# Loading the third input pair ahead of the token weights, and beginning the token product one slot early, in a fused retention and wave-MLP kernel

## Chip, cores and metric

One core of a Trainium2 chip. The metric is device time in microseconds (us), the median of some runs of one kernel. Some executions fall in a slow state with a lower granted clock (the TensorE clock that the profile records, as a share of the full one): a run more than 1.5% above the fastest of its kernel counts as slow, and ratios use the fast runs alone. A profiled run has a span that is about 1.7 us shorter than its device time; all times inside a kernel are from the start of that span. L12 is line 12 of the kernel; the change adds lines, so L340 of the kernel before is L349 after, L368 is L377, L400 is L409, L312 is L317, L322 is L331, L347 is L356, L375 is L384.

## The reference

```python
# q, k, v: (4, 8, 768, 64), float32
state = gamma * state + outer(k[t], v[t])        # per batch and head, over 768 steps
x[t]  = q[t] @ state / 8                         # heads side by side: x is (4, 768, 512)
theta = x @ w_theta
y = w_tok_r @ (x * cos(theta)) + w_tok_i @ (x * sin(theta))   # over the 768 tokens
u = x + y
out = u + max(u @ w_ch, 0)
```

## The kernel before

The retention is done in chunks of 128 tokens. A **pair** n is two chunks of one batch (3 pairs a batch, 12 in all): k and q are flipped (transposed) by TensorE into kqT, A = k q is masked by VectorE, Y = A v and the product with the state (I) add up to yT, S adds k v to the state. ScalarE or VectorE copies yT to xT; theta is a matmul of xT, ScalarE makes cosine and sine, VectorE makes z = x cos, x sin. M is the token product of one tile of 128 tokens (12 matmuls, six per weight); u = x + y; U flips u; O is the channel product; "ot" is the result. The token weights must be cast and flipped too: "w flip".

The engines take their instructions in the order in which the program writes them (the prediction gives the page and the trace line for it). What matters here are the buffers in PSUM, into which the matmuls of this kernel write, and the order in one turn of the loop, which I call **slot** n:

```python
def flip(n, name, copy=nc.vector.tensor_copy):          # 8 transposes, one copy
    ps = psum.tile([P, 2, NP, P], BF, name="kq_ps", tag="tr", bufs=2)
def x_pe(n, copy=...):   x_ps = psum.tile(..., tag="tr", bufs=2)
def moe_U(ms):           u_ps = psum.tile(..., tag="tr", bufs=2)     # read by ScalarE
def moe_O(m):            o_ps = psum.tile(..., tag="tr", bufs=2)     # read by VectorE
def w_flip(r, t0):       w_ps = psum.tile(..., tag="tr", bufs=2)     # r=0: VectorE, r=1: ScalarE
def theta(n, a):         th_ps = psum.tile(..., tag="acc", bufs=2)   # yT_ps of ret_Y has this tag too
def moe_M(m, lo, hi):    y_ps = psum.tile(..., tag="y", bufs=1)
...
# slots 4 and 5 (n), one tile "first" each; cut to the order
ret_I(n-1, 1); ret_A(n, 0); ret_mask(n, 0); ret_Y(n-1, 1); ret_S(n-1, 1)
ret_out(n-1, 0); ret_out(n-1, 1)           # yT -> xT, ScalarE
moe_M(first, 0, 2)                         # stands in the wait for xT
theta(n-1, 0); x_pe(n-1); theta(n-1, 1)    # preps(DP): q half VectorE, half GpSimd, about here
flip(n+1, "k")
ret_S(n, 0); ret_A(n, 1); ret_mask(n, 1); ret_Y(n, 0); ret_I(n, 0); moe_U(done)
moe_M(first, 2, 4)
w_tok(n)                                   # two w flips, between them on VectorE zmul(n-1, .)
moe_M(first, 4, nT); flip(n+1, "q"); moe_u(first)    # slot 5: this q flip stands behind the k flip
moe_O(done); moe_out(done)
```

Of the kernel before, what the change touches and what calls it, by code (L numbers as in the profile page):

```python
# [14 lines left out]
FT = mybir.dt.float32  # L15
BF = mybir.dt.bfloat16
# [16 lines left out]
def kernel(  # L33
# [17 lines left out]
    nc = tc.nc  # L51
# [39 lines left out]

    def load_wtok(r, t0):
        src = (moe_w_tok_r, moe_w_tok_i)[r]
        t = io.tile([P, S], FT, name="wtok", bufs=4)
        nc.sync.dma_start(out=t, in_=src[t0 * P:(t0 + 1) * P, :])
        wdma[r, t0] = t

    def loads(order):
        for what in order.split():
            if what == "th":  # L100
                load_w512("th", moe_w_theta)
            elif what == "ch":
                load_w512("ch", moe_w_ch)
            elif what[0] == "w":
                for r in range(2):
                    load_wtok(r, int(what[1:]))
            else:
                for name in "kqv":
                    load(int(what[1:]), name)

    loads("p0 th p1 w0 p2 w1 w2 p3 w3 ch p4 w4 p5 w5")


    warm = const.tile([P, dm], BF)
# [72 lines left out]
            copy(t, ps)  # L187
        st[n, name + "T"], st[n, name + "_ps"] = t, ps

    def flip_out(n, name):  # L190
        nc.vector.tensor_copy(st[n, name + "T"], st[n, name + "_ps"])

    def flip_dma(n, name):
        t = work.tile([P, 2, NP, P], BF, name="kqT", bufs=6)
# [109 lines left out]
    def x_out(n, copy):  # L304
        b, g = divmod(n, nG)
        copy(xs[b][:, 2 * g:2 * g + 2, :],
             st[n, "x_ps"].rearrange("p a j e -> p a (j e)"))

    def theta(n, a):
        th_ps = psum.tile([P, dm], FT, name="th_ps", tag="acc", bufs=2)  # L310
        for j in range(NP):
            nc.tensor.matmul(th_ps, st[n, "xT"][:, a, j, :], wth[:, j, :], start=(j == 0),  # L312
                             stop=(j == NP - 1))
        cs = work.tile([P, 2, dm], BF, name="cs", bufs=3)
        nc.scalar.activation(cs[:, 0, :], th_ps, AF.Sin, bias=halfpi, scale=1.0)  # L315
        nc.scalar.activation(cs[:, 1, :], th_ps, AF.Sin, bias=zerob, scale=1.0)  # L316
        st[n, "cs", a] = cs  # L317
# [53 lines left out]

    def moe_out(m):
        b, t0 = divmod(m, nT)
        ot = work.tile([P, dm], FT, name="ot", bufs=8)
        nc.vector.scalar_tensor_tensor(ot, mo[m]["o"], 0.0, mo[m]["u"], ALU.max, ALU.add)  # L375
        mo[m]["ot"] = ot

# [3 lines left out]

    wrow = {}

    def w_cast(t0):  # L384
        for r in range(2):
            row = work.tile([P, S], BF, name="wrow", bufs=5)
            nc.gpsimd.tensor_copy(row, wdma[r, t0])  # L387
            wrow[r, t0] = row

    def w_flip(r, t0, copy=True):  # L390
# [12 lines left out]
    def w_tok(t0):  # L403
        for r in range(2):
            w_flip(r, t0)
# [56 lines left out]
    def keep_busy(times):  # L462
        for _ in range(times):
            nc.tensor.matmul(warm_ps, warm[:, 0:P], warm, start=True, stop=True)
# [35 lines left out]
    theta(0, 1)  # L500
    flip(1, "q")
    prep(1, "v", PP)
    w_cast(0)
    x_pe(0, None)
    ret_A(1, 0)
    ret_mask(1, 0)
    x_out(0, DV.tensor_copy)
    keep_busy(3)
    ret_S(1, 0)
    state_out(1, 0)  # L510
# [1 line left out]
    ret_mask(1, 1)  # L512
    ret_Y(1, 0)
    ret_I(1, 0)
    w_flip(0, 0)
    ret_S(1, 1)
    state_out(1, 1)
    ret_I(1, 1)
    ret_Y(1, 1)
    ret_out(1, 0, AC.copy)  # L520
    ret_out(1, 1, DV.tensor_copy)
    w_flip(1, 0)
    prep(2, "k", (PL,))
    zmul(0, 0)
    flip(2, "k")
    prep(2, "q", DP)
    theta(1, 0)
    zmul(0, 1)
    theta(1, 1)
    moe_M(0, 0, 1)  # L530
    flip(2, "q")
    prep(2, "v", PP)
    w_cast(1)
    w_cast(2)
    x_pe(1, AC.copy)
    moe_M(0, 1, 2)
    ret_A(2, 0)
    ret_mask(2, 0)
    ret_S(2, 0)
    state_out(2, 0)  # L540
    ret_A(2, 1)
    ret_mask(2, 1)
    zmul(1, 0)
    ret_Y(2, 0)
    ret_I(2, 0)
    ret_I(2, 1)
    w_flip(0, 1, False)
    w_flip(1, 1, False)
    ret_Y(2, 1)
    ret_out(2, 0, AC.copy)  # L550
    ret_out(2, 1, DV.tensor_copy)
    w_out(0, 1)
    w_out(1, 1)
    zmul(1, 1)
    prep(3, "k", (PL,))
    moe_M(0, 2, 3)
    theta(2, 0)
    flip(3, "k")
    prep(3, "q", DP)
    theta(2, 1)  # L560
    moe_M(0, 3, 4)
    x_pe(2)
    w_flip(0, 2, False)
    w_out(0, 2, AC.copy)
    moe_M(1, 0, 2)
    zmul(2, 0)
    flip(3, "q")
    prep(3, "v", PP)
    w_cast(3)
    moe_M(1, 2, 4)  # L570
    zmul(2, 1)
    moe_M(0, 4, 5)


    tiles_of = {nG - 2: [], nG - 1: [0, 1]}
# [16 lines left out]
    for n in range(nG, B * nG + 1):  # L592
        mine, done = tiles_of[n], tiles_of[n - 1]
        late, two = n > nG, len(mine) > 1
        nxt = n + 1 in pairs

        if nxt and n + 1 >= K_DMA:
            flip_dma(n + 1, "k")
        if nxt and n + 1 >= Q_DMA:
            flip_dma(n + 1, "q")  # L600
        if n <= X_DMA and n + 3 in pairs:
            load(n + 3, "k")
        if n >= U_DMA:
            moe_U_dma(done[1])
        def preps(engines):
            prep(n + 1, "q", engines)
            prep(n + 1, "v", PP)
            if n in (nG, nG + 1):
                w_cast(n - nG + 4)

        if n == nG:
            nc.gpsimd.tensor_copy(wch, wdma["ch"])
        if nG + 3 < n + 1 < Q_DMA:
            preps(PP)
        if late:
            ret_I(n - 1, 1)

        if n in pairs:
            ret_A(n, 0)
            ret_mask(n, 0)  # L620
        if n == nG:
            moe_M(0, 5, nT)
            w_flip(1, 2)
            moe_u(0)
            moe_M(1, 4, nT)
            moe_u(1)
        if late:
            ret_Y(n - 1, 1)
            ret_S(n - 1, 1)
            ret_out(n - 1, 0, nc.scalar.copy)  # L630
            ret_out(n - 1, 1, nc.scalar.copy)
            state_out(n - 1, 1)
            if n < nG + 3:
                prep(n + 1, "k", (PL,))
                if n > nG + 1:
                    preps(DP)
            if n - 1 >= X_DMA:
                x_dma(n - 1)
        if n > X_DMA and n + 3 in pairs:
            load(n + 3, "k")  # L640
        if n + 3 in pairs:
            load(n + 3, "q")

        first = mine[0]
        moe_M(first, 0, 3 if two else 2)
        if late:
            theta(n - 1, 0)
            if n - 1 < X_DMA:
                x_pe(n - 1)
            if n == nG + 1:  # L650
                preps(DP)
            theta(n - 1, 1)
        if two:
            moe_M(first, 3, nT)
            moe_u(first)
        for name, limit in (("k", K_DMA), ("q", Q_DMA)):
            if nxt and nG + 1 < n + 1 < limit and (n > nG + 1 or name == "k"):
                flip(n + 1, name)
        if n + 1 >= K_DMA and not two:
            moe_M(first, 2, 4)  # L660
        if n + 3 in pairs:
            load(n + 3, "v")
        for t in stores_in(n):
            store(t)
        if n + 1 >= U_DMA:
            moe_U_dma(first)

        if n in pairs:
            ret_S(n, 0)
            state_out(n, 0)  # L670
            ret_A(n, 1)
            ret_mask(n, 1)
            ret_Y(n, 0)
            ret_I(n, 0)
        if n < U_DMA:
            moe_U(done)
        if n == nG:
            prep(n + 1, "k", (AC,))
            preps(DP)
        if n == nG or n + 1 < K_DMA and not two:  # L680
            moe_M(first, 2, 4)
        early_z = late and n < nG + 3
        if early_z and n > nG + 1:
            zmul(n - 1, 0)
        if n < nG + 3:
            w_tok(n - nG + 3)
        if early_z:
            zmul(n - 1, 0 if n == nG + 1 else 1)
        if not two:
            moe_M(first, 4, nT)  # L690
            if n == nG + 1:
                flip(n + 1, "q")
            moe_u(first)
            if n == nG + 1:
                zmul(n - 1, 1)
        elif n in pairs:
            moe_M(mine[1], 0, nT)
        if n + 2 in pairs and n > nG + 1:
            prep(n + 2, "k", (AC,))
        if n + 2 in pairs and n + 2 >= Q_DMA:  # L700
            prep(n + 2, "q", PP)
            prep(n + 2, "v", PP)
        if two and n in pairs:
            moe_u(mine[1])
        for i, t in enumerate(done):
            if n == nG:
                flip(n + 1, "kq"[i])
            moe_O(t)
            moe_out(t)
        if late and not early_z:  # L710
            zmul(n - 1, 0)
            zmul(n - 1, 1)
        if n not in pairs:
            moe_M(mine[1], 0, nT)
            moe_u(mine[1])
# [43 lines left out]
```

## Time and profile before

| kernel before | |
|---|---|
| time, median of 3 runs | 168.55 us (168.35 to 169.74) |
| span of the profiled run | 166.5 us, granted clock 1.00 |
| prologue, to A of pair 3 | 38.25 us |
| slots 3, 4, 5, 6 | 10.16, 10.22, 10.20, 7.76 us |
| slot 7 begins | 76.59 us |

Slot boundaries are read off TensorE in order of time: the first state product (L245) of each slot. The lines are in the prediction. Two more: all that TensorE waited for theta and for Y over the whole run, from the list of waits (engine, line, releaser, us in total, times, longest):

```profile
PE th_ps L312 <- ACT xT L285: 0.3, 1, 0.3
PE yT_ps L231 <- ACT cs L316: 0.3, 1, 0.3
```

### The profile page before, as it was taken

The page shows a single profiled execution, that of the slowest core. Times are in us where ns is not written, and L with a number is a line of the kernel's source. Part 1 is how long each engine was busy: PE and PEld are TensorE (multiplying, and loading weights), DVE is VectorE, ACT ScalarE, POOL GpSimd, SP SyncE. Part 2 cuts the span into 40 slices and gives each one's busy share as a digit, 9 for nine tenths or more (in the row PEclk, how much of TensorE's full clock was granted, in tenths as well). Part 3 has the DMA queues.
Part 4 walks back from the last instruction along what each step waited for, and adds up shares of the span by engine and source line. Part 5 has one row for each costly group of instructions (what it writes and reads, how often), then busy time and mean ns, then how long its engine had stood idle before and what let it go on. Part 6 is the DMA issues. An engine that isn't in the chain of part 4 may idle for free.

```text
span 166.5 us, 4614 instructions
## 1 busy us (share of the span) xinstructions
PE 155.2 (93%) x1933; PEld 87.2 (52%) x1959; DVE 102.4 (61%) x137; ACT 79.1 (48%) x137; POOL 66.6 (40%) x82
## 2 busy tenths in 40 slices
PE   6969897899999999999999999999999999999991
PEld 2345664664755667555555554455545444444460
DVE  2257798878686699939446464584554736334442
ACT  7216568371819467687847827447083350000010
POOL 6275959786685877771442703600000000000000
PEclk9999999999999999999999999999999999999999
DMA  4999999999999999999999999998996161753343
GB/s 122 309 345 307 326 326 354 286 328 317 293 311 349 277 278 331 309 202 250 206 231 298 163 242 203 195 233 168 266 145 185 32 189 32 231 115 100 106 141 135
DMA packets 68901, 38.45 MB, mean 231 GB/s; under 512 B 26256, under 2 KB 63376, under 8 KB 68880
## 3 DMA queue, kind: packets, MB, share of 16 engines
q1 hardware_dynamic: 68736, 38.02, 90.2%
q8 instruction: 15, 0.25, 0.7%
q10 hardware_dynamic: 144, 0.13, 0.2%
q14 instruction: 6, 0.05, 0.1%
HBM read 25.69 MB, written 6.29 MB: 192 GB/s over the span
## 4 chain that ended last, share of the span: by engine, by line
PE 77%; DVE 12%; DMA 3%; issue 3%; ACT 1%; POOL 1%; DVEq 0%; SPq 0%; POOLq 0%
PE y_ps L340 33%; PE o_ps L368 12%; PE th_ps L312 11%; PE at_ps L208 4%; PE yT_ps L231 4%; DVE at L215 4%; DMA pair<-in_q_dram 3%; PE yT_ps L245 3%; PE st_ps L262 3%; PE kq_ps L183 3%; DVE z L322 2%; PE w_ps L393 2%; DVE kqT L187 2%; PE y_ps L420 2%; DVE kqb L175 1%
## 5 line engine op out<-in xcount | busy, mean ns | idle before, releaser
L340 PE MATMUL y_ps<-z,wtr 128*128 128x512 bf16 x133 | 50.5, 379 | 1.1
L340 PE MATMUL y_ps<-z,wti 128*128 128x512 bf16 x122 | 46.2, 379 | 0.4 <-issue 0.2
L347 DVE TENSOR_TENSOR u<-y_ps,x_sb 128x512 bf16<-128x512 f32 x23 | 15.9, 690 | 27.0 <-PE y_ps L340 27.0
L215 DVE TENSOR_TENSOR at<-at_ps,maskp 128x1024 bf16<-128x1024 f32 x24 | 29.3, 1221 | 4.6 <-PE at_ps L208 4.6
L175 POOL TENSOR_TENSOR kqb<-pair,qscp 128x512 bf16<-128x512 f32 x17 | 19.3, 1150 | 28.9 <-DMA pair<-in_q_dram 26.0
L175 POOL TENSOR_TENSOR kqb<-pair,vscp 128x512 bf16<-128x512 f32 x24 | 26.6, 1131 | 5.0 <-DMA pair<-in_v_dram 4.9
L285 ACT CAST xT<-yT_ps 128x512 bf16<-128x512 f32 x20 | 13.5, 739 | 30.0 <-PE yT_ps L231 29.9
L375 DVE SCALAR_TENSOR_TENSOR ot<-o_ps,u 128x512 f32<-128x512 f32 x23 | 15.9, 690 | 13.2 <-PE o_ps L368 13.2
L312 PE MATMUL th_ps<-wth,xT 128*128 128x512 bf16 x93 | 23.2, 379 | 0.5 <-ACT xT L285 0.3
L368 PE MATMUL o_ps<-wch,uT 128*128 128x512 bf16 x92 | 22.8, 379 | 0.3
L340 PEld LDWEIGHTS <-wtr 128*128 128x128 bf16 x138 | 13.5, 98 | 13.8
L276 ACT CAST stbd<-st_ps 64x256 bf16<-64x256 f32 x40 | 14.7, 368 | 12.5 <-PE st_ps L262 12.0
L340 PEld LDWEIGHTS <-wti 128*128 128x128 bf16 x138 | 13.5, 98 | 13.6 <-ACT wti L400 0.4
L315 ACT ACTIVATE cs<-th_ps,halfpi 128x512 bf16<-128x512 f32 x24 | 16.5, 689 | 7.0 <-PE th_ps L312 6.6
L322 DVE TENSOR_TENSOR z<-cs,x_sb 128x1024 bf16<-128x1024 bf16 x24 | 18.8, 808 | 0.1
L316 ACT ACTIVATE cs<-th_ps,zerob 128x512 bf16<-128x512 f32 x24 | 16.5, 687 | 0.0
L312 PEld LDWEIGHTS <-xT 128*128 128x128 bf16 x96 | 8.9, 98 | 11.0 <-ACT xT L285 1.0
L368 PEld LDWEIGHTS <-uT 128*128 128x128 bf16 x92 | 8.8, 98 | 10.5 <-issue 0.6
L208 PE MATMUL at_ps<-kqT 64*64 64x128 bf16 x384 | 10.6, 221 | 2.6 <-DVE at L215 1.8
L430 ACT COPY uT<-u_ps 128x384 bf16<-128x384 bf16 (+1 forms) x2 | 0.7, 372 | 25.5 <-PE u_ps L429 25.5
L187 DVE COPY kqT<-kq_ps 128x1024 bf16<-128x1024 bf16 x14 | 9.6, 688 | 4.2 <-PE kq_ps L183 4.1
L387 POOL CAST wrow<-wtok 128x768 bf16<-128x768 f32 x12 | 10.5, 902 | 0.3 <-DMA wtok<-in_moe_w_tok_i_dram 0.2
(61 smaller groups left out, 164.4 us busy)
## 6 DMA issues: line engine op xcount, KB each, us to landing
pair<-in_k_dram SPq DMA_DIRECT2D x12, 512.0 KB, 6.7
pair<-in_q_dram SPq DMA_DIRECT2D x12, 512.0 KB, 7.7
pair<-in_v_dram SPq DMA_DIRECT2D x12, 512.0 KB, 8.2
out_dram<-ot SPq DMA_DIRECT2D x23, 256.0 KB, 2.6
wtok<-in_moe_w_tok_r_dram SPq DMA_DIRECT2D x6, 384.0 KB, 6.4
wtok<-in_moe_w_tok_i_dram SPq DMA_DIRECT2D x6, 384.0 KB, 5.8
w<-in_moe_w_theta_dram SPq DMA_DIRECT2D x1, 1024.0 KB, 8.3
w<-in_moe_w_ch_dram SPq DMA_DIRECT2D x1, 1024.0 KB, 8.5
```

Source lines behind the costliest of these rows:

```text
L175: engines[two].tensor_mul(dst[:, two], src[:, two], _bcast_last(sc[:, 2 * g + two], D))
L208: nc.tensor.matmul(at_ps[half, par, j, :], kT[rows, two, j, half], qT[rows, :, j, half], start=(j == 0), stop=(j == NP - 1), skip_group_ch ...
L215: nc.vector.tensor_mul(at.rearrange("p a j t -> p (a j) t"), at_ps.rearrange("p a j t -> p (a j) t"), _bcast_mid(maskp[:, two].rearrange(" ...
L276: nc.scalar.copy(stbd[(c + 1) % 2][sl, :, sl], st_ps[b][sl])
L312: nc.tensor.matmul(th_ps, st[n, "xT"][:, a, j, :], wth[:, j, :], start=(j == 0), stop=(j == NP - 1))
L315: nc.scalar.activation(cs[:, 0, :], th_ps, AF.Sin, bias=halfpi, scale=1.0)
L316: nc.scalar.activation(cs[:, 1, :], th_ps, AF.Sin, bias=zerob, scale=1.0)
L322: nc.vector.tensor_mul(zs[b][:, c], st[n, "cs", a], _bcast_mid(xs[b][:, c, :], 2))
L340: nc.tensor.matmul(y_ps, wT[r][:, s0, t0 * P:(t0 + 1) * P], zs[b][:, s0, r, :], start=(s0 == 0 and r == 0), stop=(s0 == nT - 1 and r == 1))
L347: nc.vector.tensor_add(u, mo[m]["y"], xs[b][:, t0, :])
L368: nc.tensor.matmul(o_ps, mo[m]["uT"][:, j, :], wch[:, j, :], start=(j == 0), stop=(j == nD - 1))
L375: nc.vector.scalar_tensor_tensor(ot, mo[m]["o"], 0.0, mo[m]["u"], ALU.max, ALU.add)
```

## The change

Its intent: start the third pair before the token weights have come, finish M of tiles 0 and 1 before the loop, and then always begin the next tile's M (four matmuls) at the end of a slot, with the q flip among them, so that the flip's wait for its data is filled. More buffers for the weights (4 to 6) are paid for with fewer for ot (8 to 5); cs gets one more (3 to 4).

```diff
-        t = io.tile([P, S], FT, name="wtok", bufs=4)
+        t = io.tile([P, S], FT, name="wtok", bufs=6)
-    loads("p0 th p1 w0 p2 w1 w2 p3 w3 ch p4 w4 p5 w5")
+    loads("p0 th p1 p2 w0 w1 w2 p3 ch w3 p4 w4 p5 w5")
-        ot = work.tile([P, dm], FT, name="ot", bufs=8)
+        ot = work.tile([P, dm], FT, name="ot", bufs=5)
... prologue: pair 2 moved ahead of every w flip; M of tiles 0 and 1 whole (cut) ...
@@ the loop
-        moe_M(first, 0, 3 if two else 2)
+        if two or n == nG:
+            moe_M(first, 0, 3)
         if late:
             theta(n - 1, 0)
... preps(DP) and flip(n + 1, "q") taken out of the middle of the slot ...
         if not two:
-            moe_M(first, 4, nT)
-            if n == nG + 1:
-                flip(n + 1, "q")
+            moe_M(first, 3 if n == nG else 4, nT)
             moe_u(first)
+            if nG < n < nG + 3:
+                zmul(n - 1, 0)
+            if n < nG + 3:
+                w_tok(n - nG + 3)
+            if nG < n < nG + 3:
+                zmul(n - 1, 1)
+            if n == nG:
+                flip(n + 1, "k", nc.scalar.copy)
+            if n == nG + 3:
+                flip(n + 1, "q")
@@
         for i, t in enumerate(done):
             moe_O(t)
             moe_out(t)
+            if n < nG + 3 and i == 0:
+                preps(DP)
+        if n < nG + 3:
+            moe_M(first + 1, 0, 2)
+            flip(n + 1, "q")
+            moe_M(first + 1, 2, 4)
```

More of the change, by code (lines that the diff above doesn't have):

```diff
@@ L188, in flip, with flip_out @@
         st[n, name + "T"], st[n, name + "_ps"] = t, ps
-    def flip_out(n, name):
-        nc.vector.tensor_copy(st[n, name + "T"], st[n, name + "_ps"])
+    def flip_out(n, name, copy=nc.vector.tensor_copy):
+        copy(st[n, name + "T"], st[n, name + "_ps"])
     def flip_dma(n, name):
@@ L309, in theta, with theta_mm @@
     def theta(n, a):
-        th_ps = psum.tile([P, dm], FT, name="th_ps", tag="acc", bufs=2)
+        theta_mm(n, a)
+        sines(n, a)
+    def theta_mm(n, a, tag="acc"):
+        th_ps = psum.tile([P, dm], FT, name="th_ps" if tag == "acc" else "y_ps", tag=tag,
+                          bufs=2 if tag == "acc" else 1)
         for j in range(NP):
@@ L313, in theta, with sines @@
                              stop=(j == NP - 1))
-        cs = work.tile([P, 2, dm], BF, name="cs", bufs=3)
+        st[n, "th", a] = th_ps
+    def sines(n, a):
+        th_ps = st[n, "th", a]
+        cs = work.tile([P, 2, dm], BF, name="cs", bufs=4)
         nc.scalar.activation(cs[:, 0, :], th_ps, AF.Sin, bias=halfpi, scale=1.0)
@@ L382, with w_cast @@
     wrow = {}
-    def w_cast(t0):
+    def w_cast(t0, copy=nc.gpsimd.tensor_copy):
         for r in range(2):
             row = work.tile([P, S], BF, name="wrow", bufs=5)
-            nc.gpsimd.tensor_copy(row, wdma[r, t0])
+            copy(row, wdma[r, t0])
             wrow[r, t0] = row
@@ L502 @@
     prep(1, "v", PP)
-    w_cast(0)
     x_pe(0, None)
@@ L507 @@
     x_out(0, DV.tensor_copy)
+    prep(2, "k", (PL,))
     keep_busy(3)
@@ L514 @@
     ret_I(1, 0)
-    w_flip(0, 0)
     ret_S(1, 1)
@@ L518 @@
     ret_I(1, 1)
+    flip(2, "k", None)
+    prep(2, "q", DP)
     ret_Y(1, 1)
@@ L521 @@
     ret_out(1, 1, DV.tensor_copy)
-    w_flip(1, 0)
-    prep(2, "k", (PL,))
-    zmul(0, 0)
-    flip(2, "k")
-    prep(2, "q", DP)
-    theta(1, 0)
-    zmul(0, 1)
-    theta(1, 1)
-    moe_M(0, 0, 1)
+    flip_out(2, "k", AC.copy)
+    keep_busy(1)
     flip(2, "q")
     prep(2, "v", PP)
-    w_cast(1)
-    w_cast(2)
-    x_pe(1, AC.copy)
-    moe_M(0, 1, 2)
+    theta(1, 0)
     ret_A(2, 0)
     ret_mask(2, 0)
+    zmul(0, 0)
+    x_pe(1, None)
+    theta_mm(1, 1, "y")
     ret_S(2, 0)
     state_out(2, 0)
+    sines(1, 1)
+    w_cast(0)
     ret_A(2, 1)
     ret_mask(2, 1)
-    zmul(1, 0)
+    x_out(1, DV.tensor_copy)
     ret_Y(2, 0)
@@ L546 @@
     ret_I(2, 1)
-    w_flip(0, 1, False)
-    w_flip(1, 1, False)
+    w_flip(0, 0, False)
     ret_Y(2, 1)
-    ret_out(2, 0, AC.copy)
-    ret_out(2, 1, DV.tensor_copy)
-    w_out(0, 1)
-    w_out(1, 1)
+    ret_out(2, 0, DV.tensor_copy)
+    ret_out(2, 1, AC.copy)
+    w_out(0, 0)
+    w_flip(1, 0)
+    w_cast(1)
+    theta(2, 0)
+    zmul(0, 1)
+    theta(2, 1)
+    zmul(1, 0)
     zmul(1, 1)
+    x_pe(2)
     prep(3, "k", (PL,))
-    moe_M(0, 2, 3)
-    theta(2, 0)
-    flip(3, "k")
-    prep(3, "q", DP)
-    theta(2, 1)
-    moe_M(0, 3, 4)
-    x_pe(2)
-    w_flip(0, 2, False)
-    w_out(0, 2, AC.copy)
+    moe_M(0, 0, 3)
+    w_flip(0, 1)
+    w_flip(1, 1)
+    moe_M(0, 3, 4)
+    zmul(2, 0)
+    zmul(2, 1)
+    flip(3, "k", None)
+    flip_out(3, "k", AC.copy)
+    prep(3, "q", PP)
+    prep(3, "v", PP)
+    w_cast(2, AC.copy)
+    moe_M(0, 4, nT)
     moe_M(1, 0, 2)
-    zmul(2, 0)
     flip(3, "q")
-    prep(3, "v", PP)
-    w_cast(3)
-    moe_M(1, 2, 4)
-    zmul(2, 1)
-    moe_M(0, 4, 5)
+    moe_u(0)
+    moe_M(1, 2, nT)
+    w_flip(0, 2)
+    w_flip(1, 2)
+    moe_u(1)
     tiles_of = {nG - 2: [], nG - 1: [0, 1]}
@@ L612 @@
             nc.gpsimd.tensor_copy(wch, wdma["ch"])
+            w_cast(n - nG + 3)
         if nG + 3 < n + 1 < Q_DMA:
@@ L620 @@
             ret_mask(n, 0)
-        if n == nG:
-            moe_M(0, 5, nT)
-            w_flip(1, 2)
-            moe_u(0)
-            moe_M(1, 4, nT)
-            moe_u(1)
         if late:
@@ L634 @@
                 prep(n + 1, "k", (PL,))
-                if n > nG + 1:
-                    preps(DP)
             if n - 1 >= X_DMA:
@@ L649 @@
                 x_pe(n - 1)
-            if n == nG + 1:
-                preps(DP)
             theta(n - 1, 1)
@@ L655 @@
             moe_u(first)
-        for name, limit in (("k", K_DMA), ("q", Q_DMA)):
-            if nxt and nG + 1 < n + 1 < limit and (n > nG + 1 or name == "k"):
-                flip(n + 1, name)
-        if n + 1 >= K_DMA and not two:
-            moe_M(first, 2, 4)
+            if nxt and n + 1 < Q_DMA:
+                flip(n + 1, "q")
+        if nG < n < nG + 3:
+            flip(n + 1, "k")
         if n + 3 in pairs:
@@ L678 @@
             prep(n + 1, "k", (AC,))
-            preps(DP)
-        if n == nG or n + 1 < K_DMA and not two:
-            moe_M(first, 2, 4)
-        early_z = late and n < nG + 3
-        if early_z and n > nG + 1:
-            zmul(n - 1, 0)
-        if n < nG + 3:
-            w_tok(n - nG + 3)
-        if early_z:
-            zmul(n - 1, 0 if n == nG + 1 else 1)
-        if not two:
-            moe_M(first, 4, nT)
-            if n == nG + 1:
+        if not two:
+            moe_M(first, 3 if n == nG else 4, nT)
+            moe_u(first)
+            if nG < n < nG + 3:
+                zmul(n - 1, 0)
+            if n < nG + 3:
+                w_tok(n - nG + 3)
+            if nG < n < nG + 3:
+                zmul(n - 1, 1)
+            if n == nG:
+                flip(n + 1, "k", nc.scalar.copy)
+            if n == nG + 3:
                 flip(n + 1, "q")
-            moe_u(first)
-            if n == nG + 1:
-                zmul(n - 1, 1)
         elif n in pairs:
@@ L705 @@
         for i, t in enumerate(done):
-            if n == nG:
-                flip(n + 1, "kq"[i])
             moe_O(t)
             moe_out(t)
-        if late and not early_z:
+            if n < nG + 3 and i == 0:
[4 more added lines that the diff above has]
+            moe_M(first + 1, 2, 4)
+        if late and n > nG + 2:
             zmul(n - 1, 0)
```

## The prediction

> **What bounds the kernel now.** I read the page first, then TensorE in order of time, then the chain of work that ended last, then a table of stretches cut where a new slot starts (a slot is one turn of the loop over n from 3 on, and begins with the product of a state, L245, or in slot 3 with A of pair 3, L208).
>
> ```profile
> PE 155.2 (93%) x1933; PEld 87.2 (52%) x1959; DVE 102.4 (61%) x137; ACT 79.1 (48%) x137; POOL 66.6 (40%) x82
> PE   6969897899999999999999999999999999999991
> ...
> 14.77:38.25 23.48, 20.96 (x335) 13.93 (x340) 19.57 (x26) 14.28 (x25) 18.77 (x19) 1.00 1.09 325
> 38.25:48.41 10.16, 9.80 (x131) 5.94 (x133) 7.91 (x11) 4.19 (x6) 7.19 (x7) 1.00 1.04 307
> 48.41:58.63 10.22, 9.75 (x168) 6.62 (x168) 7.18 (x10) 6.49 (x12) 7.27 (x9) 1.00 1.10 310
> 58.63:68.83 10.20, 9.93 (x168) 6.56 (x169) 10.19 (x14) 7.52 (x13) 8.12 (x8) 1.00 1.09 309
> 68.83:76.59 7.76, 7.66 (x120) 4.20 (x120) 5.00 (x7) 6.01 (x10) 5.01 (x5) 1.00 1.07 211
> ```
>
> TensorE is the bound, and from 66 us to the end it hardly pauses, so what the stretch ahead of that loses or wins goes whole into the end time. The last five lines are the prologue from the first theta, and slots 3, 4, 5, 6 (columns: length, then busy PE, PEld, DVE, ACT, POOL, clock, DMA). A lone 128x512 matmul is shown as 0.379 us, but the next one starts 0.215 us later, so busy is not work. Counting by starts (theta or O of a tile, 4 matmuls, 0.86; M of a tile, 12 matmuls, 2.59; a flip 0.45; A or Y 0.24; S 0.25; a state product 0.22; the two w flips 0.67; x 0.45), slots 4 and 5 hold about 9.3 us of work in 10.2, slot 6 7.3 in 7.76, and the prologue some 18.4 in 23.48. Thus at most 5 us are to be had in the prologue and 2 to 3 in the slots.
>
> How little a slot loses today comes from what is placed in its waits. Slot 4 on TensorE:
>
> ```profile
> 49.21 0.42 PE L262 MATMUL st_ps<-kqb 64*64 64x64 bf16 x16
> 49.78 0.38 PE L340 MATMUL y_ps<-z,wti 128*128 128x512 bf16 x1 [0.16 <-issue]
> 50.00 0.38 PE L340 MATMUL y_ps<-z,wtr 128*128 128x512 bf16 x1
> 50.22 0.38 PE L340 MATMUL y_ps<-z,wti 128*128 128x512 bf16 x1
> 50.43 1.03 PE L312 MATMUL th_ps<-wth,xT 128*128 128x512 bf16 x4
> ...
> 54.12 0.41 PE L231 MATMUL yT_ps<-at,kqb 64*64 64x128 bf16 x14 [0.26 <-ACT cs L316]
> ...
> 57.32 0.61 PE L183 MATMUL kq_ps<-ident,kqb 128*128 128x128 bf16 x8
> 57.77 1.03 PE L368 MATMUL o_ps<-wch,uT 128*128 128x512 bf16 x4
> ```
>
> Four matmuls of M fill the time in which ScalarE copies yT to xT (`49.41 1.34` for the two copies, so the first is there at about 50.1), before theta at 50.43. Y waits for the sines of the second theta. The last four of M and the q flip lie between the w flips and O. What happens where that filling is thin is in the chain of slot 5, where the q flip already stands earlier:
>
> ```profile
> 65.91 1.54 DVE z L322
> 67.44 0.48 DVE wtr L400
> 67.92 0.04 issue
> 67.97 1.02 PE o_ps L368 x4
> ```
>
> O follows the copy of the w flip on VectorE at once: o_ps, w_ps, u_ps, x_ps and kq_ps share the tag "tr" with two buffers, and each use waits for the reader of the second last.
>
> **What the Trainium skill says.** "TensorE: Matmul & The Clock Gate", Step-by-step: what each phase is for: matmuls stay in program order, only weight loads are pulled ahead; its Architectural detail section has VectorE and ScalarE as strict FIFOs. The trace agrees: nothing passed Y at 54.12 although work stood behind it. So a matmul moved behind a wait cannot fill it. "Perfetto Trace Analysis", Identifying the Most-Contended Engine: matmul busy share is no measure of the distance to the limit; here 0.379 us shown against 0.215 between starts agrees. "SBUF — State Buffer", Who interferes with whom: VectorE and GpSimd contend for one port pair, as an exclusive lock; the z at 65.91 took 1.54 us beside GpSimd's q preparation, where two z at 99.07 took 1.28 together. I take it as a risk of 0.4 to 0.9 us per z that meets GpSimd.
>
> **The change part by part.**
>
> *Loads.* Two w tiles (0.79 MB) no longer stand before pair 2; at the 325 GB/s of the prologue that is 2.4 us. GpSimd begins k of pair 2 at 21.86 and q at 23.67, both on the DMA's landing, so after the change about 19.4 and 21.3. w0 falls behind one more pair (1.57 MB, 4.8 us): landing 20.05 becomes about 24.9, w1 and w2 follow at 27 to 30. Pair 3 keeps its place.
>
> *Prologue.* I placed the instructions by hand, from their durations. Y(1,1) is at 22.0 as before; its xT is there at 23.3, flip of 2q is done at 23.3 (after its preparation at 22.8) and copied at 24.2. A(2,0) starts at 24.3 instead of 27.38. Then masks of 1.23 us gate: A(2,1) 26.1, Y(2,1) 27.9, its xT 29.1, theta(2) 29.2 to 30.9. M(0) can only begin when w0 is flipped and z of tiles 1 and 2 are made by VectorE (29.5 to 31.4), so at about 31.4; z(2,0) and z(2,1) come at 34.3 and 34.9, M(1) ends at 38.4 and with two more w flips A(3,0) starts at 39.1, or 39.9 if the z meet GpSimd. Before it was 38.25, but with M(0) lacking 2 matmuls, M(1) lacking 4 and one w flip: 6 x 0.215 + 0.33 = 1.62, so 39.87 on the same footing. Gain: 0 to 0.8, I take **-0.4**. The earlier pair mostly turns into later weights; TensorE still has about 4 us without work between 21 and 30.
>
> *Slot 3.* A(3,0), then M(2) waits for the ScalarE copy of the last w flip (0.95 after the start), 6 matmuls to 2.1; S, A, Y, u to 3.3; M to 4.6; w flips to 5.25; u (0.69) and w copy (0.55) on VectorE to 5.9, only then the k flip, 6.4; O 7.25; next O waits for ScalarE's copy of the k flip, 7.65 to 8.5; M of tile 3, q flip (0.45), M: 10.66. Before 10.16, for 0.1 less work: **+0.4**.
>
> *Slots 4 and 5, from the first instruction.* First S ends at 0.95, theta must wait for xT until 1.7 because M no longer stands there; sines end at 5.4 (before 5.7), Y, state, u to 6.2, M(4 to 6) ends at 7.1. Now VectorE in order: u 7.3 to 8.0, z 8.6, w copy 9.05. The w flips end at 7.8 and O needs the buffer of the first: idle to 9.1, **1.3**. O ends 9.95, VectorE's ot 10.8, its half of q 11.4; M(0 to 2) of the next tile fills to 10.8, then the q flip waits to 11.45, **0.65**; flip 0.45, M 0.86: 12.75. Against 10.2 for the same work that is 2.55 a slot, **+5.1** for two.
>
> *Slot 6.* It starts with 4 of M done, so its work is 1.72 less and it should take 6.04. But theta waits to 1.7 and Y for the sines until 5.3 with nothing beside it; then u 0.25, M 0.86, flip 0.45, O 0.86 to 7.95: **+1.9**.
>
> *Buffers.* ot has 5 for 8. Tile 8 reuses the buffer of tile 3, whose store is issued at 107.23 and lands 2.3 to 4.9 us later, while ot of tile 8 now runs at 108.07. VectorE waits some 2.5 us, with idle time behind it (2.44 before the next u); left over on TensorE perhaps **+0.5**.
>
> Sum: -0.4 + 0.4 + 5.1 + 1.9 + 0.5 = 7.5, that is 176.0. As the prologue is the least sure and its slack of 5 us is the one place of gain, I move to **175.2 us**.
>
> **The rivals.** *First: the prologue wins, and the slots hold.* VectorE was full through slot 5 (10.19 busy of 10.20); if that was the true bound, moving k flips to ScalarE and the q half to the slot's end would let it run through, and 3 to 4 us come out of the prologue: 165 to 167. Against it: VectorE's amount in slots 4 and 5 is unchanged, and u now stands before z and the w copy, so they start later. *Second: the waits in the slots are right, but the prologue gains 3 us* as A(2,0) does: 171.5 to 173. For it: A(2,0) is 3 us earlier; against it the later w0 and the chain of z. *Third: DMA bound.* Its share is over 1 up to slot 6; if loads set the pace, order on TensorE counts for little and the time stays within 1%. Against it: pair 5 lands at 49.8 to 53.8 and its k flip is at 52.6, its q flip at 57.3; TensorE names no DMA as releaser. *Fourth: z meets GpSimd in both slots*, each lengthening the wait of O: 177 to 178.5.
>
> **Range and chances.** The sum's sure part is 7.0 in slots 4 to 6, from rows whose order is fixed by the program; the prologue may give back up to 3.6 before the result comes under 2% (171.9). Range 170.0 to 178.5. Slower by over 2% 0.78, within 2% 0.16, faster 0.06.
>
> **What would show it.** Right: slots 4 and 5 at 12 to 13 us; an idle of over 1 us before O released by the w copy, of 0.5 before the q flip released by VectorE's q half, and of 0.6 before theta released by xT; slot 6 near 8; A(2,0) near 24.3 and A(3,0) near 39.5. Wrong: slots of 10 to 10.5, or A(3,0) before 37, either of which takes the loss away.

## The result

The changed kernel is correct and takes 178.47 us (median of 4 runs, 177.71 to 181.48; the last was slow), the kernel before on the same chips 168.93 us. The ratio of the fast runs is 1.0546, interval 1.0476 to 1.0617: slower. Ratios here and below are the mean time of one kernel's fast runs over that of the other's of the same rounds, so not quite the ratio of the medians that I quote.

First the page of the changed kernel (busy shares, then TensorE's busy tenths in 40 slices), and its table of the prologue and slots 3 to 6, cut where its own slots begin:

```profile
PE 156.3 (88%) x1933; PEld 87.2 (49%) x1960; DVE 101.7 (58%) x135; ACT 81.7 (46%) x140; POOL 64.8 (37%) x81
PE   7679888969898788776999999999999999999990
...
14.73:41.51 26.78, 23.34 (x348) 14.96 (x352) 20.91 (x26) 16.23 (x27) 19.45 (x18) 1.00 1.08 322
41.51:52.63 11.12, 9.84 (x128) 5.65 (x129) 7.81 (x10) 5.30 (x7) 7.70 (x9) 1.00 1.09 311
52.63:65.55 12.92, 10.26 (x167) 6.56 (x168) 8.64 (x12) 6.39 (x12) 9.45 (x10) 1.00 0.88 238
65.55:78.14 12.59, 10.25 (x167) 6.58 (x168) 8.09 (x12) 7.32 (x13) 5.92 (x5) 1.00 0.62 182
78.14:86.22 8.08, 6.24 (x112) 3.76 (x113) 3.59 (x5) 5.88 (x10) 2.04 (x2) 1.00 0.90 208
```

TensorE's unbroken row of nines begins after 19 slices (84 us); before, it began after 8 (33 us). Slots 4 and 5 hold the same matmuls as before and last 12.92 and 12.59 us; VectorE, full in slot 5 before, is now busy 8.09 us of it; and DMA falls from a share over 1 to 0.62. Everybody waits: the sign of a chain, not of a full engine.

Slot 4 of the changed kernel on TensorE, only the lines with a wait (in brackets: idle before it, and what ended it), then the same two waits in slot 6:

```profile
54.42 1.04 PE L317 MATMUL th_ps<-wth,xT 128*128 128x512 bf16 x3 [0.58 <-ACT xT L285]
...
58.12 0.41 PE L231 MATMUL yT_ps<-at,kqb 64*64 64x128 bf16 x14 [0.26 <-ACT cs L325]
...
61.51 1.02 PE L377 MATMUL o_ps<-wch,uT 128*128 128x512 bf16 x4 [0.89 <-ACT wti L409]
...
64.23 0.62 PE L183 MATMUL kq_ps<-ident,kqb 128*128 128x128 bf16 x8 [0.84 <-DVE kqb L175]
...
79.92 1.90 PE L317 MATMUL th_ps<-wth,xT 128*128 128x512 bf16 x7 [0.82 <-ACT xT L285]
...
83.47 0.41 PE L231 MATMUL yT_ps<-at,kqb 64*64 64x128 bf16 x14 [0.91 <-ACT cs L325]
```

Four waits, 2.57 us in one slot, where slot 4 of before had 0.16 and 0.26. How far such a slot varies can be read off, as slots 4 and 5 stand unedited in four traces (this one, e1, e9 and e10 below): slot 4 took 12.64 to 13.38 us and slot 5 12.59 to 13.40, the q flip's wait 0.52 to 1.33, the other waits the same to 0.01. So a few tenths between two traces are no finding where that wait is in play. After slot 6 the two kernels run in step: slot 7 begins at 86.22 instead of 76.59, 9.63 us later, and the last slot's first product at 140.23 instead of 130.59, 9.64 later.

| part (from the traces) | before | after | cost, for equal work | predicted |
|---|---|---|---|---|
| prologue, to A of pair 3 | 38.25, + 1.62 of work not yet done | 41.51 | +1.64 | -0.4 |
| slot 3 | 10.16, + 0.10 of work | 11.12 | +0.86 | +0.4 |
| slots 4 and 5 | 20.42 | 25.51 | +5.09 | +5.1 |
| slot 6 | 7.76, - 1.72 of work | 8.08 | +2.04 | +1.9 |
| slots 7 on, and end | 89.9 | 90.4 | +0.5 | +0.5, for another reason |

The last half microsecond lies behind TensorE's last matmul, in the last store; the predicted wait of ot for its buffer is there, 1.84 us on VectorE, but slot lengths on TensorE around it are equal to those of before (10.47 and 10.93 in both), so it cost nothing there:

```profile
119.37 1.32 DVE L384 SCALAR_TENSOR_TENSOR ot<-o_ps,u 128x512 f32<-128x512 f32 x2 [1.84 <-PE yT_ps L231]
```

(The profile names TensorE; by the order of the program this ot waits for the store of its buffer. Two runs below bear it out: with five buffers and the old loop, e2, the same ot waits 1.86 us; with eight and the new loop, e1, 0.17. The half microsecond behind TensorE's last matmul is not theirs: e1 has it too, 0.4 us, and e2 has not.)

### The profile page after: what moved, and what is told of

It is laid out like the page before. It is cut to its first block, busy times and chain, and to the rows that moved or that the text cites. A ratio compares the mean times of both kernels' runs of the same rounds, so it can differ in the third digit from the quotient of the medians.

```text
span 176.6 us, 4617 instructions
## 1 busy us (share of the span) xinstructions
PE 156.3 (88%) x1933; PEld 87.2 (49%) x1960; DVE 101.7 (58%) x135; ACT 81.7 (46%) x140; POOL 64.8 (37%) x81
## 4 chain that ended last, share of the span: by engine, by line
PE 65%; DMA 9%; DVE 8%; ACT 7%; issue 4%; POOL 2%; SPq 1%; DVEq 0%; ACTq 0%
PE y_ps L349 31%; PE o_ps L377 11%; PE th_ps L317 8%; DMA pair<-in_q_dram 5%; DMA w<-in_moe_w_theta_dram 5%; DVE z L331 3%; PE yT_ps L231 3%; PE at_ps L208 2%; PE yT_ps L245 2%; PE kq_ps L183 2%; ACT cs L325 2%; ACT xT L285 2%; PE st_ps L262 2%; DVE kqb L175 2%; ACT cs L324 2%
## 5 line engine op out<-in xcount | busy, mean ns | idle before, releaser
L349 PE MATMUL y_ps<-z,wti 128*128 128x512 bf16 x125 | 47.4, 379 | 0.6 <-ACT wti L409 0.2
L175 POOL TENSOR_TENSOR kqb<-pair,qscp 128x512 bf16<-128x512 f32 x18 | 20.9, 1175 | 33.6 <-DMA pair<-in_q_dram 33.6
L175 POOL TENSOR_TENSOR kqb<-pair,vscp 128x512 bf16<-128x512 f32 x24 | 25.5, 1083 | 8.7 <-DMA pair<-in_v_dram 6.1
L317 PE MATMUL th_ps<-wth,xT 128*128 128x512 bf16 x86 | 22.0, 379 | 2.4 <-ACT xT L285 2.0
L324 ACT ACTIVATE cs<-th_ps,halfpi 128x512 bf16<-128x512 f32 x23 | 15.8, 688 | 6.6 <-PE th_ps L317 6.5
L331 DVE TENSOR_TENSOR z<-cs,x_sb 128x1024 bf16<-128x1024 bf16 x24 | 18.1, 788 | 0.0
L325 ACT ACTIVATE cs<-th_ps,zerob 128x512 bf16<-128x512 f32 x23 | 15.8, 686 | 0.0
L183 PE MATMUL kq_ps<-ident,kqb 128*128 128x128 bf16 x120 | 9.5, 219 | 3.9 <-DVE kqb L175 1.6
L231 PE MATMUL yT_ps<-at,kqb 64*64 64x128 bf16 x384 | 10.8, 218 | 1.6 <-ACT cs L325 1.4
```

The lines of the kernel that those rows point to most:

```text
L175: engines[two].tensor_mul(dst[:, two], src[:, two], _bcast_last(sc[:, 2 * g + two], D))
L231: nc.tensor.matmul(yT[a][par * D:(par + 1) * D, j, :], vp[half, two, h * D:(h + 1) * D], at[half, par, j, :], start=(two == 0 and j == 0), ...
L317: nc.tensor.matmul(th_ps, st[n, "xT"][:, a, j, :], wth[:, j, :], start=(j == 0), stop=(j == NP - 1))
L324: nc.scalar.activation(cs[:, 0, :], th_ps, AF.Sin, bias=halfpi, scale=1.0)
L325: nc.scalar.activation(cs[:, 1, :], th_ps, AF.Sin, bias=zerob, scale=1.0)
L331: nc.vector.tensor_mul(zs[b][:, c], st[n, "cs", a], _bcast_mid(xs[b][:, c, :], 2))
```

## The experiments

**Theory.** The slots lose by their own order: O stands directly behind the w flips in the same two buffers, the q flip waits for a half of q that VectorE makes only after ot, and M no longer stands before theta. **Rivals.** The slots are slow because the new prologue hands over late; beginning M ahead is by itself what costs; VectorE's amount or the sines set the slot, so that any wait that is taken away comes back elsewhere. A second question is the prologue, which I had got wrong. Time of the changed kernel for comparison: 178.47 us, fast runs 177.71 to 178.63.

### Which half costs: slots alone, prologue alone

`e1_slots_only`: prologue, loads and buffers of before, with the new loop.

```diff
# on the kernel before
+    moe_M(0, 5, nT); w_flip(1, 2); moe_u(0); moe_M(1, 4, nT); moe_u(1)   # ahead of the loop
... the loop is the changed kernel's (without its w_cast of w3, done in this prologue) ...
```

> Prologue, load order and buffers of the kernel before, with the four reordered slots 3 to 6 (M of tiles 0 and 1 finished ahead of slot 3). Theory (the new order of the slots costs the time by itself: slot 3 +0.9, slots 4 and 5 +5.1, slot 6 +2.0 in the two traces): about 8 us over the kernel before, 176 to 177.5 us, ratio 1.045 to 1.05; slots 4 and 5 at 12.5 to 13 us. Rival (the slots are slow only because the new prologue hands data over late): under 171 us, slots of 10.2 to 10.7 us.

`e2_prologue_only`: the changed kernel with the loop of before.

```diff
# on the changed kernel: the old loop put back, but for these lines of it
-        if n == nG:
-            moe_M(0, 5, nT); w_flip(1, 2); moe_u(0); moe_M(1, 4, nT); moe_u(1)
```

> Prologue, load order and buffers of the changed kernel, with slots 3 to 6 ordered as in the kernel before. Theory (the prologue lost 1.6 us in the trace, where I predicted a gain of 0.4): 170 to 171 us, ratio 1.007 to 1.015, slots 4 and 5 at about 10.2 us. Rival (earlier pair is worth something once the slots do not spoil it): 167 to 168 us, ratio under 0.998.

Measured: slots alone 177.91 us, ratio 1.0546 (1.0492 to 1.06); prologue alone 169.58 us, ratio 1.0048 (1.0004 to 1.0091). Slots 4 and 5 of each, from their tables, first of slots alone, then of prologue alone:

```profile
51.27:64.39 13.12, 10.39 (x169) 6.49 (x168) 8.84 (x12) 6.38 (x12) 8.91 (x9) 1.00 1.06 291
64.39:76.99 12.60, 10.36 (x170) 6.58 (x169) 8.10 (x12) 7.33 (x13) 8.28 (x8) 1.00 0.68 200
```

```profile
50.31:60.53 10.22, 9.96 (x170) 6.63 (x169) 7.18 (x10) 6.44 (x12) 7.73 (x8) 1.00 1.13 313
60.53:70.59 10.06, 9.87 (x170) 6.58 (x168) 9.96 (x14) 7.29 (x13) 6.99 (x6) 1.00 1.10 300
```

The slots are slow behind either prologue and fast with the old order behind either. The first rival is out. Slots alone came out a little above what I expected, prologue alone below it: it costs half a per cent in the timed runs, less than its trace suggested (169.96 us was the profiled run, the highest of its four). The two halves do not add: slots alone cost as much as the whole change. In that run's trace, with the loads and the order of before, A of pair 3 starts at 40.80 us, where 38.25 + 1.62 gives 39.87. So some 0.9 of the prologue's 1.64 comes with finishing tiles 0 and 1 ahead of the loop (M waits 0.64 us for z there), and not with the earlier pair; these are single traces.

### Which edit of the slot: w flips first, q by GpSimd, both

`e3_w_before_M` puts the w flips and z ahead of M's last part:

```diff
+            if nG < n < nG + 3: zmul(n - 1, 0)
+            if n < nG + 3: w_tok(n - nG + 3)
+            if nG < n < nG + 3: zmul(n - 1, 1)
             moe_M(first, 3 if n == nG else 4, nT)
             moe_u(first)
-            (the same three lines)
```

> The changed kernel, but in slots 3 to 5 the two w flips and the two z stand before the last matmuls of M, not behind them, so that M lies between the w flips and O and VectorE need not wait for M. Theory (O waits for the copy of a w flip because nothing lies between them): the idle of 0.9 us before O goes, slots 4 and 5 fall by about 1.2 us each and slot 3 by 0.5, in all 2.5 to 3 us, 175.5 to 176 us. Rival (the slots are set by the sines before Y and by VectorE's amount, so the wait only moves to the next point, the q flip): less than 1 us.

`e4_q_gpsimd`:

```diff
-                preps(DP)
+                preps(PP)
```

> The changed kernel, but GpSimd makes both halves of q in slots 3 to 5, not VectorE the first half after ot. Theory (the q flip at the end of the slot waits for VectorE's q half, 0.84 and 0.52 us in slots 4 and 5 and some 0.3 in slot 3): these waits go, 1.6 to 2 us off, about 176.7 us; GpSimd has the time, it made its half 10 us before the flip. Rival (GpSimd's second half delays v and k of the next pair, or takes VectorE's port): no gain, 178 us or more.

`e7_w_first_q_gpsimd` has both edits.

> The two edits together: w flips before the last of M, and q by GpSimd. Theory (alone, the first only moved the wait from O to the q flip, 1.1 us there): now both go, slots 4 and 5 at about 11.5 us (12.7 and 12.0 with one edit each), 174.5 to 175.3 us. Rival (the edits overlap in what they save): no better than the better of the two, 176 us.

| | median us | ratio to before | slots 3, 4, 5, 6 |
|---|---|---|---|
| changed | 178.47 | 1.0546 | 11.12, 12.92, 12.59, 8.08 |
| w flips first | 176.97 | 1.0481 | 11.06, 12.71, 12.72, 8.07 |
| q by GpSimd | 176.18 | 1.0422 | 10.87, 12.00, 11.90, 8.08 |
| both | 175.44 | 1.0405 | 11.06, 11.65, 11.43, 8.09 |

With the w flips first the slots did not shorten by more than two traces differ: the rival was right about the slots, though not with its "less than 1 us" for the whole. TensorE in slot 4 of that run, the waits at the second w flip and at the q flip:

```profile
58.44 0.49 PE L402 MATMUL w_ps<-ident,wrow 128*128 128x128 bf16 x6 [0.34 <-ACT uT L370]
...
62.72 0.62 PE L183 MATMUL kq_ps<-ident,kqb 128*128 128x128 bf16 x8 [1.11 <-DVE kqb L175]
```

The wait before O is gone, the one before the q flip is 1.11 instead of 0.84 (within what it varies by in unedited slots), and a new one stands at the w flip, which now follows u's flip in the buffers. (The run is 1.5 us faster all the same: its prologue, not edited, reached A of pair 3 at 40.27 instead of 41.51. More on this under the prologue.) With q by GpSimd the 0.84 and 0.52 us go, and the slots shorten by 0.92 and 0.69. With that done the first edit is worth 0.35 and 0.47 a slot: O's wait of 0.89 is gone and 0.34 at the w flip has come (the intervals of the timed ratios overlap). Two waits in a row on one chain: taking away the first alone only lets the second be met sooner.

### Which of the two moves: M ahead, or the q flip at the end

`e5_M_not_ahead`:

```diff
-        if two or n == nG:
-            moe_M(first, 0, 3)
+        moe_M(first, 0, 3 if two or n == nG else 2)
-            moe_M(first, 3 if n == nG else 4, nT)
+            moe_M(first, 3 if n == nG else 2, nT)
-            moe_M(first + 1, 0, 2)
             flip(n + 1, "q")
-            moe_M(first + 1, 2, 4)
```

> The changed kernel, but M of tiles 3 to 5 is not begun in the slot ahead: its first four matmuls stand before theta again, the rest in the middle; the q flip stays at the slot's end. Theory (each matmul of M fills one wait or another, and the end of the slot has as much to fill as its head): the waits before theta go (0.6, 0.6 and 0.8 us) but those before the q flip grow by what M(0 to 2) hid there (0.86 a slot), and A of the next slot waits for the copy of the q flip (some 0.6 a slot): within 1 us of the changed kernel, 177.5 to 179 us. Rival (the move of M is what costs): 171 to 173 us.

`e6_q_flip_back` (q prepared where it was before, flipped between the w flips and O; M's four matmuls whole at the end):

```diff
-                preps(DP)                    # after ot
+                preps(DP)                    # slot 3: after k's; slot 4: between the thetas; slot 5: after k's
+        if nG < n < nG + 3:
+            flip(n + 1, "q")                 # ahead of O (slot 3: between its two)
-            moe_M(first + 1, 0, 2); flip(n + 1, "q"); moe_M(first + 1, 2, 4)
+            moe_M(first + 1, 0, 4)
```

> The changed kernel with M of tiles 3 to 5 still begun in the slot ahead, but q prepared early and flipped between the w flips and O, as in the kernel before. Theory: the wait before the q flip goes (0.84, 0.52, 0.24) and the q flip fills half of the wait before O (0.45 of 0.9); slots 4 and 5 at about 11 us, in all 3 to 4 us off the changed kernel, 174 to 175 us; the waits before theta (0.6, 0.6, 0.8) stay. Rival (the flip's place is innocent, M's is to blame): 177 us or more.

Measured: M not ahead 182.24 us, ratio 1.0783 (one of four runs slow); q flip back 176.84 us, ratio 1.0492, slots 10.96, 11.90, 11.90, 8.08.

The q flip's way back gave 1.6 us, half of what I expected, and the trace says why. TensorE at the q flip of slot 4 in that run:

```profile
61.10 0.61 PE L183 MATMUL kq_ps<-ident,kqb 128*128 128x128 bf16 x8 [0.89 <-ACT wti L409]
```

It is the very 0.89 us that O waited. The q flip uses the tag "tr" too, so it does not fill the wait, it takes it over. Only work that needs none of these buffers (M, theta, A, Y) can fill it; in the kernel before it is M's last four matmuls.

Taking M back, with the q flip left at the end, was far worse than the changed kernel, beyond both theory and rival. As expected the q flip then waits 1.70 and 1.38 us and A of the next slot 0.56 for its copy. The rest is the clock. Stretches of 2 us of that run, columns as in the tables above; the eighth entry, after POOL, is the granted clock:

```profile
60.00:62.00 2.00, 1.11 (x14) 0.75 (x12) 2.00 (x4) 0.80 (x1) 1.37 (x2) 1.00 1.10 307
62.00:64.00 2.00, 0.52 (x3) 0.02 (x1) 2.00 (x3) 0.00 (x0) 1.61 (x2) 1.00 0.46 132
...
66.00:68.00 2.00, 2.00 (x42) 1.32 (x35) 1.23 (x1) 1.37 (x3) 1.63 (x2) 0.50 0.77 230
68.00:70.00 2.00, 2.00 (x11) 0.88 (x9) 0.00 (x0) 0.56 (x3) 1.08 (x2) 0.70 1.09 382
```

TensorE is busy 1.63 of 4 us, and within 2 us its clock is 0.50 for about 3.5 us; the same again at 80 us. A busy TensorE at half clock looks like a full one.

`e12_e5_kept_busy` tests that:

```diff
# on e5
+                fill = psum.tile([P, dm], FT, name="y_ps", tag="y", bufs=1)
+                for _ in range(6):
+                    nc.tensor.matmul(fill, warm[:, 0:P], warm, start=True, stop=True)
             flip(n + 1, "q")                 # slots 4 and 5
```

> The run with M not ahead, whose trace showed a granted clock of 0.50 for some 3.5 us after the longest waits (0.9 before O and 1.7 before the q flip, 1.6 us of work in 4), plus six idle matmuls (1.3 us) in the wait before the q flip of slots 4 and 5. Theory (the sparse stretch lowers the clock, and the half clock costs more than the wait): clock 1.00 through the slots, slots 5 and 6 shorter by about 2 us each, 178 to 179.5 us although work was added. Rival (the clock falls for another reason, or the added work lengthens the slots): 182 us or more.

Measured 180.86 us, ratio 1.0706 (e5: 1.0783), and through slots 4 to 6 the clock is 1.00 in the trace, here at the same place:

```profile
62.00:64.00 2.00, 1.60 (x9) 0.55 (x7) 1.89 (x3) 0.00 (x0) 1.34 (x1) 1.00 0.37 98
...
66.00:68.00 2.00, 1.95 (x25) 1.01 (x20) 1.04 (x1) 1.91 (x4) 0.56 (x1) 1.00 0.92 284
```

Slot 4, where the clock had held, is 13.76 us in both; slots 5 and 6 are 13.77 and 9.57 instead of 15.30 and 10.44. So the sparse stretch does lower the clock in this trace, and matmuls of no use shorten these two slots; I had put it at 2 us a slot and it was 1.5 and 0.9. (In the timed runs the medians lie 1.4 us apart, less than the 2.7 to 4.2 I expected, and the intervals overlap.) The four parts at full clock sum to 46.94 us against 44.71 of the changed kernel: with the q flip at the end, beginning M ahead is a **gain** of 2.2 us, not the culprit. I had expected within 1 us there. In slot 4 the 0.58 before theta went, but 0.86 was added before the q flip and 0.56 before A: 0.84 more, which is just the 13.76 against 12.92. I had named all three and let them cancel.

### Filling the waits: `e8_waits_filled`

```diff
# on the changed kernel; preps(PP) as in e4
+        else:
+            moe_M(first, 4, nT); moe_u(first)       # before theta
             ret_mask(n, 1)
+            if nG < n < nG + 3: w_tok(n - nG + 3)   # before Y, which waits for the sines
+            if n == nG + 3:     flip(n + 1, "q")
             ret_Y(n, 0)
... after u's flip, slots 4 and 5:
+                zmul(n - 1, 0); zmul(n - 1, 1)
+                moe_M(first + 1, 0, 2)              # before O
```

> The changed kernel with M still begun in the slot ahead, but with something in each wait of slots 4 to 6: the rest of M stands before theta, the w flips (slot 6: the q flip) before Y, which waits for the sines anyway, the first two pairs of the next tile's M before O, and GpSimd makes q. Theory (the change loses only by empty waits, not by beginning M early): slots 4 and 5 at 9.7 to 10.2 us, slot 6 at 7 to 7.4, 6.5 to 7.5 us off the changed kernel, 171 to 172 us, what is left being the prologue and slot 3. Rival (VectorE's order u, mask, x copy makes new waits): slots of 11 us, 174 us.

Measured 172.96 us, ratio 1.0257. Slots 4, 5 and 6:

```profile
51.83:62.25 10.42, 10.10 (x169) 6.54 (x168) 7.33 (x11) 6.44 (x12) 8.90 (x10) 1.00 0.94 279
62.25:72.67 10.42, 10.10 (x169) 6.54 (x168) 7.40 (x11) 7.40 (x13) 6.40 (x7) 1.00 1.06 314
72.67:80.30 7.63, 6.62 (x113) 3.64 (x112) 3.88 (x5) 5.88 (x10) 3.59 (x4) 1.00 0.80 164
```

5.5 us come back with M still begun ahead and the q flip still at the end, a little less than expected (u's flip now waits 0.32 for the w copy, and slot 6's O 0.68 for uT). The loss was the empty waits, not the moves as such. Nor did other waits take their place: VectorE is busy 7.33 and 7.40 us of 10.42, and in slots 4 and 5 Y no longer waits for the sines. So the third rival is out too.

### The prologue

In the traces of the nine kernels with this same prologue (the changed one, e2 to e8 and e12) A of pair 3 starts between 40.27 and 41.59 us, though their programs are the same up to there. What differs is VectorE's z of tiles 4 and 5, 2.13 to 2.98 us for the two. In the changed kernel, VectorE and GpSimd:

```profile
34.35 2.88 DVE L331 TENSOR_TENSOR z<-cs,x_sb 128x1024 bf16<-128x1024 bf16 x2
```

```profile
34.20 2.49 POOL L175 TENSOR_TENSOR kqb<-pair,qscp 128x512 bf16<-128x512 f32 x2 [0.61 <-DMA pair<-in_q_dram]
```

`e9_z_alone` makes GpSimd wait for those z:

```diff
+    gate = const.tile([P, 8], BF)
+    nc.gpsimd.tensor_copy(gate, zs[0][:, 5, 1, 0:8])
     prep(3, "q", PP)
```

> The changed kernel, but GpSimd first reads eight columns of the last z of batch 0 before it prepares q of pair 3, so that it does not run beside z of tiles 4 and 5 in the prologue. Theory (the part of the prologue that I missed is VectorE's z slowed by GpSimd: 2.88 us for two in the changed kernel, 1.28 for two where GpSimd rests; in seven traces of this same prologue A of pair 3 starts at 40.3 to 41.6 us, the later the slower these two z): the two z take 1.3 us, M(0) ends 1.6 us earlier, but the q flip comes at 37.9 instead of 38.6 at best; A of pair 3 at 40.4 to 40.9, 0.6 to 1.1 us off. Rival (the loads' landing sets it): z fast, but A of pair 3 still at 41.3 to 41.6.

`e10_loads_as_before`:

```diff
-    loads("p0 th p1 p2 w0 w1 w2 p3 ch w3 p4 w4 p5 w5")
+    loads("p0 th p1 w0 p2 w1 w2 p3 ch w3 p4 w4 p5 w5")
```

> The changed kernel with w0 loaded before pair 2 again, all else as changed. Theory (the prologue of the changed kernel runs along pair 2's chain): A of pair 2 starts 2 to 2.5 us later (24.6 becomes about 27), A of pair 3 1.5 to 2.5 us later, 179.5 to 181 us. Rival (the prologue is held by the weights, z and GpSimd, so the earlier pair is worth nothing): A of pair 3 within 0.5 us of 41.5, 178 to 179 us.

With GpSimd held back: 177.16 us, ratio 1.0485. VectorE and GpSimd of that run:

```profile
34.42 1.28 DVE L331 TENSOR_TENSOR z<-cs,x_sb 128x1024 bf16<-128x1024 bf16 x2
```

```profile
35.92 2.04 POOL L175 TENSOR_TENSOR kqb<-pair,qscp 128x512 bf16<-128x512 f32 x2
```

Both are at their own pace, z 1.6 us faster, q 0.45 us faster, and A of pair 3 starts at 40.74, 0.77 earlier, as expected: the q flip comes later because q begins later (it waits 0.58 us for GpSimd). By itself 40.74 proves little, as it lies inside the 40.27 to 41.59 above; the times of z and q are the evidence. With w0 loaded first again: 182.33 us (two of its four runs slow; the fast ones 180.10 and 181.14), A of pair 2 at 27.23 instead of 24.56 and A of pair 3 at 43.79. That is 2.3 us later, but not all of it is the pair's place: GpSimd takes up pair 2's k 2.0 us later (22.05 instead of 20.03), TensorE waits for it, and then this trace has the low clock too, as in e5 (two stretches of 4 us; the eighth entry is the clock, which is 0.50 from 23.2 to 26.6 us):

```profile
23.15 1.01 PE L183 MATMUL kq_ps<-ident,kqb 128*128 128x128 bf16 x8 [1.54 <-POOL kqb L171]
...
20.00:24.00 4.00, 2.46 (x64) 1.95 (x63) 1.93 (x3) 1.30 (x4) 1.29 (x2) 0.90 1.09 269
24.00:28.00 4.00, 3.67 (x54) 2.47 (x54) 2.12 (x4) 2.27 (x4) 4.00 (x4) 0.67 0.89 307
```

So with this order of work, loading the pair later costs 2.3 us, of which a part is the clock. Measured against the kernel before, the order of work as a whole gives the earlier pair's gain away again: M(0) waits 0.74 and 0.86 us for z in the changed kernel. Whether w0 coming late has a part in it, no run shows. Of the 1.64, z beside GpSimd makes 0.8 (e9) and finishing tiles 0 and 1 ahead of the loop some 0.9 (e1); the two may overlap, as both are waits of M(0) for z, and I did not separate them.

### A version faster than both: `e11_before_q_gpsimd`

```diff
# on the kernel before, slots 4 and 5
-                preps(DP)
+                preps(PP)
```

> The kernel before with one word changed: GpSimd makes both halves of q in slots 4 and 5, where VectorE is busy 10.19 of 10.20 us in slot 5. Theory (VectorE is the tight engine of slot 5, TensorE waits for it by some 0.5 us): slot 5 0.3 to 0.6 us shorter, ratio 0.996 to 0.999. Rival (GpSimd's longer work meets z and the k preparation comes later): ratio 1.000 to 1.004.

Measured over five rounds: 167.67 us against 168.86, ratio 0.9937 (0.9904 to 0.9970). Slot 5:

```profile
59.37:69.14 9.77, 9.66 (x168) 6.59 (x168) 8.58 (x13) 7.30 (x13) 7.86 (x8) 1.00 0.96 281
```

VectorE is busy 8.58 us and no longer full; the slot is 0.43 shorter, slot 4 unchanged (10.21), as expected. The record calls this "same", as it is under 2%, but the interval lies wholly below 1. The whole is more than slot 5 gives: 0.43 us would be a ratio of 0.9975, just outside the interval, so where the rest comes from is not shown. The trace does not tell: it is of the slowest of the six runs, and its slot 3, which the edit does not touch, took 11.05 us instead of 10.16.

## Why the prediction was right or wrong

The direction, the place and the mechanism were right: 5.09 us in slots 4 and 5 against a predicted 5.1, 2.04 in slot 6 against 1.9, and undoing the order of the slots gives back all but half a per cent. The sums are closer than they deserve: the same slots 4 and 5 took 25.51 to 26.21 us in four traces, a cost of 5.1 to 5.8, so a match to 0.01 is luck. So is the range: the measured 178.47 us lies 3.3 above the point and 0.03 inside the range, and the fast runs go up to 178.63. Of the signs that I had named, A of pair 3, "near 39.5", came at 41.51, and "over 1 us before O" holds only as the prediction counts, by starts (1.05); the profile shows 0.89 idle. Step by step:

- **theta waiting for xT.** Right: 0.58, 0.57 and 0.82 us.
- **Y waiting for the sines in slot 6.** Right: 0.91 us.
- **O waiting for the w copy.** Right in kind, wrong in detail. I had O take the buffer of the first w flip and wait 1.3 us for VectorE. The trace has it released by ScalarE's copy of the second w flip, after 0.89 us; VectorE's copy (61.19, 0.55 us long) ended only after O had begun. So O did not get the buffer that I had counted on; why, the trace does not show. The order u, z, copy on VectorE, which I made much of, did not set this wait; putting z and the w flips first (e3) won nothing by it.
- **The q flip waiting for VectorE's q half.** Right in kind, 0.84 and 0.52 against 0.65; it was the costlier wait of the two to remove, 1.6 us in the two slots (e4). The sum of both was predicted at 1.95 a slot. The profile shows 1.73 and 1.41 idle, but that leaves out the end of the matmul before. Counted by starts, as the prediction does, it is 1.05 + 1.00 and 1.05 + 0.69.
- **Slot 3.** Mis-sized: 0.86 for 0.4. TensorE waits 0.58 there for the k flip's buffer, 0.24 for O's and 0.24 for q, the last as VectorE's q half took 1.50 us beside GpSimd.
- **Prologue.** The step that failed: "Gain: 0 to 0.8, I take -0.4". It lost 1.64 in the trace, and in e2's timed runs 0.5%, some 0.8 us. I had named z meeting GpSimd as a risk of 0.4 to 0.9 us per z and placed A of pair 3 at 39.1, or 39.9 with it; z took 0.8 us more each, and pair 3's k was taken up at 32.55 us, where I had left it at its old 31.30 (it varies: 31.14 to 32.66 in the traces of this prologue, 32.04 in e1, which has the loads of before). And I took the finishing of tiles 0 and 1 as bare work of 1.62 us, where e1 shows some 0.9 of waiting with it. Worse, I then moved the point from 176.0 down to 175.2 on the thought that the prologue could only surprise with a gain. Against slot 3's 0.5 it was the larger error.
- **Fewer ot buffers.** The wait came (1.84 us on VectorE), its cost on TensorE did not. The 0.5 us that the end did come later is not theirs: e1 has most of it with eight buffers.
- **Not foreseen:** that idle stretches can lower the clock. It did not touch the changed kernel's profiled run (1.00 up to 168 us). Whether its one slow run (181.48 us, clock 0.985) was such a case is open; that run left no trace.

## What to carry to other kernels

A filler matmul is worth what the wait is that it stands in, and only if it needs none of the buffers that are waited for: before moving one, list the waits it covers now and those it will cover then. Work that shares a small pool of buffers does not fill that pool's wait, it inherits it. And when one of two successive waits is removed without gain, remove the second before giving up on the first. Before reading a few tenths off one trace, look how far an unedited stretch differs from trace to trace: here up to 0.8 us in a slot.

## What the Trainium skill lacked or had wrong

- "TensorE: Matmul & The Clock Gate", HAM oscillation: the rule given is to have no idle gap of TensorE over about 3.4 us. In e5 the longest single wait ahead of the half clock was 1.70 us, with 0.89 shortly before it: 1.63 us busy of 4 was enough for a clock of 0.50 over some 3.5 us. Six matmuls, 1.3 us, in that wait kept it at 1.00. In e10's prologue a wait of 1.54 us went ahead of another half clock, 23.2 to 26.6 us; in e9 0.89 and 1.31 in one slot left it at 1.00. Its next section, on short idles between groups of matmuls, is the nearer one, but gives no amount of idle.
- No page that I used says that in a shared tag with two buffers a following user takes over the wait of the one that it was put ahead of: 0.89 us before O (changed kernel), the same 0.89 before the q flip (e6).
- "SBUF — State Buffer", Who interferes with whom, names the contention of VectorE and GpSimd but not its size for bf16 products: here two z took 2.88 us beside GpSimd's q and 1.28 alone, and GpSimd's two halves 2.49 and 2.04. In this the runs agree with the page.
